# One engine instead of two for the lower parts of the second expert weights, after each change of expert

## The chip, the cores and the metric

The kernel runs on one core of a Trainium2 chip. The metric is the device time of one execution in microseconds, the median of several runs. Five engines work side by side on the core, each with an instruction queue of its own that it follows in order: TensorE (in the rows PE, its weight loads PEld), VectorE (DVE), ScalarE (ACT), GpSimd (POOL) and SyncE (SP), which here issues most of the DMAs. GpSimd issues the gathers and scatters by index as DMAs of its own. An engine waits for another through semaphores.

## The reference

The program is a chain of three parts, on float32 data:

```python
attn_out = _attn_ref(q, k, v)                 # 8 batches, 8 heads, 576 rows, 64 columns
x = attn_out.transpose(0, 2, 1, 3).reshape(4608, 512)

# mixture of experts: 8 experts, w1[e] is 512 x 1024, w2[e] is 1024 x 512
do_compute = x @ w_skip > 0
xc = x[do_compute]
e_idx = np.argmax(xc @ w_gate, axis=1)        # each row goes to one expert
for e in range(8):
    h = np.maximum(xc[e_idx == e] @ w1[e], 0.0)
    y[e_idx == e] = gate_w * (h @ w2[e])
out[do_compute] = xc + y

# then a rational MLP over all 4608 rows: g = P(x @ w_in) / Q(x @ w_in); g @ w_out
```

Only the part with the experts is touched by the change.

## The kernel before

A float32 product is made on TensorE in three passes: each operand is split into a higher part (rounded to the type that TensorE reads at its full rate) and a lower part, the difference; the passes are higher x higher, higher x lower and lower x higher. The helper `split(hi, lo, s, on_pool)` does it: ScalarE casts `s` to `hi` (L835), and then VectorE, or GpSimd if `on_pool` is set, subtracts `hi` from `s` into `lo` (L837).

The rows of the experts are sorted into slots of 256 rows, at most 25 slots (`MAXS`), each of one expert. `slot(i, kd, ch)` is emitted once for each slot, under run-time branches: `kd` says whether both halves of 128 rows are filled (2, a full slot) or one (1, a half slot), and `ch` what comes after it: 0, the same expert stays; 1, another expert follows; 2, this was the last one. A slot goes like this:

- gathers of the gates (L930, GpSimd);
- layer 1 on TensorE (L870, in a half slot L904 with transposes at L913), the relu and its split into `hh` and `hl` (L876 and L877, in a half slot L835 and L837); in a full slot also layer 2 of the second half (`layer2(1, ...)`, L886) and its store (L893 on VectorE, the scatter L894 on GpSimd);
- the transposes of the next slot's rows (L855) and their split into `xth` and `xtl`;
- gathers of the rows of the slot after that (L849, GpSimd);
- layer 2 of the first half (`layer2(0, ...)`, L886);
- if the expert stays: two pairs of blocks of the MLP's weights are loaded and converted (L796 to L813), around the store;
- if it changes: `split_w1` for eight blocks of 128 columns, from the staging tile `hold` into `w1h` and `w1l`; then the store; then `split_w2` for eight blocks, from the staging tile `w2s` into `w2h` and `w2l`; then `load_next(i + 1)`, by which SyncE loads the expert after the next into `hold` (L827) and `w2s` (L832, 2 MB each).

So the weights of an expert are loaded while the slots of the one before are computed, and split at the change. `w2s` can be loaded anew only when all eight blocks are split. In layer 2 the passes of a block f are `hh` x `w2h`, `hh` x `w2l` and `hl` x `w2h`, in this order (L885). Within the sections of a slot the order on each engine is that of the code (`tc.manual_schedule()`).

Which engine subtracts for `w2l` is decided in `split_w2`: VectorE the blocks 0, 2, 4, 6 and GpSimd the blocks 1, 3, 5, 7. It is called at two places: once before the first slot's work (L973), and at each change of expert (L1016). With 8 experts there are 7 changes.

Of the kernel before, what the change touches and what calls it, by code (L numbers as in the profile page):

```python
# [128 lines left out]
def load_block(nc, hold, xd, b):  # L129
    return nc.sync.dma_start(out=held_x(hold), in_=xd[b * TB:(b + 1) * TB, :].rearrange("(p j) d -> p j d", p=P))  # L130


def load_in(nc, hold, wc_in, f2):
    nc.sync.dma_start(out=held_wi(hold, f2), in_=wc_in[:, f2 * 2 * P:(f2 + 1) * 2 * P].rearrange("(k p) f -> p k f", p=P))
# [646 lines left out]
def experts(tc, w1, w2, w_in, w_out, wc_in, wc_out, xd, gd, ident, logits, sidx, gates, etab, xtab, kind, change, pair, early, hold, xts, hr, wos, w2s, phs, ahead, hs, av, ab, R, dbg=None):  # L781
# [5 lines left out]
    with ExitStack() as st:  # L787
# [6 lines left out]
        def convert_load(c, u):  # L794
            for m in range(2):
                nc.sync.dma_start(out=raws[2 * u + m], in_=src[m][:, c])  # L796

        def convert(c, u):
            parts = []
            for m in range(2):  # L800
                lo, hi = raws[2 * u + m][:, 0, :, 0], raws[2 * u + m][:, 0, :, 1]
                sq = cv.tile([P, CW], F32, name=f"cvs{m}")
                nc.scalar.activation(sq, hi.bitcast(F32), AF.Square)  # L803
                parts.append((lo, hi, sq, cv.tile([P, CW], I32, name=f"cvt{m}")))
            for lo, hi, sq, t in parts:
                nc.vector.tensor_scalar(out=t, in0=hi, scalar1=3, scalar2=0x3FFFFFFF, op0=ALU.logical_shift_left, op1=ALU.bitwise_and)
            for lo, hi, sq, t in parts:
                nc.vector.scalar_tensor_tensor(out=t, in0=hi, scalar=-0x40000000, in1=t, op0=ALU.bitwise_and, op1=ALU.bitwise_or)
            for lo, hi, sq, t in parts:
                nc.vector.scalar_tensor_tensor(out=t, in0=lo, scalar=29, in1=t, op0=ALU.logical_shift_right, op1=ALU.bitwise_or)  # L810
            for m, (lo, hi, sq, t) in enumerate(parts):
                nc.vector.scalar_tensor_tensor(out=sq, in0=sq, scalar=2.0 ** -30, in1=t.bitcast(F32), op0=ALU.is_ge, op1=ALU.mult)
                nc.sync.dma_start(out=dst[m][:, c], in_=sq.unsqueeze(1))  # L813
# [4 lines left out]
        w2h, w2l = wp.tile([P, KF, DM], F32R, name="w2h"), wp.tile([P, KF, DM], F32R, name="w2l")  # L818
# [15 lines left out]
        def split(hi, lo, s, on_pool):  # L834
            nc.scalar.copy(hi, s)  # L835
            eng = nc.gpsimd if on_pool else nc.vector
            eng.tensor_tensor(out=lo, in0=s, in1=hi.bitcast(F32), op=ALU.subtract)  # L837

        def split_w1(c, on_pool):
            sl = (slice(None), slice(None), slice(c * P, (c + 1) * P))  # L840
            split(w1h[sl], w1l[sl], w1s[sl], on_pool)

        def split_w2(f):
            split(w2h[:, f, :], w2l[:, f, :], w2s[:, f, :], f % 2 == 1)

        def gather(i):
            for a in range(2):
                col = 2 * i + a
                g = nc.gpsimd.indirect_dma_start(xrow[i % 3][a], None, xd, bass.IndirectOffsetOnAxis(ap=sidx[:, col:col + 1], axis=0), bounds_check=NT - 1, oob_is_err=False)  # L849
                tc.declare_no_dep(g.ins, group="scatters", reason="every slot reads and writes rows of its own")  # L850
# [28 lines left out]
        def layer2(a, hh, hl, py=None):  # L879
            if py is None:  # L880
                py = ps["y"][a]
            ts_ = slice(a * P, (a + 1) * P)
            n = 0
            for f in range(KF):
                for h, w in ((hh, w2h), (hh, w2l), (hl, w2h)):  # L885
                    nc.tensor.matmul(out=py, lhsT=h[:, f, ts_], rhs=w[:, f, :], start=(n == 0), stop=(n == 3 * KF - 1))  # L886
                    n += 1
            return py
# [31 lines left out]
        def get(tab, i, top):  # L920
            return nc.values_load(tab[0:1, i:i + 1], min_val=0, max_val=top, skip_runtime_bounds_check_because="the table holds sums of results of comparisons")

        def pair_at(i, u):
            c = nc.values_load(pair[0:1, 1 + u, i:i + 1], engines=[ET.SP], min_val=0, max_val=NPAIR - 1, skip_runtime_bounds_check_because="the table holds numbers of pairs, bounded by a minimum")
            return bass.ds(c, 1)

        def gather_gates(i):
            for a in range(2):
                col = 2 * i + a
                nc.gpsimd.indirect_dma_start(gates[:, col:col + 1], None, gd, bass.IndirectOffsetOnAxis(ap=sidx[:, col:col + 1], axis=0), bounds_check=NT - 1, oob_is_err=False)  # L930

        def load_next(i):
            e = expert(xtab, i, [ET.SP])
            load_w1(e)
            load_w2(e)
# [6 lines left out]
        def part1_full(i, hh, hl):  # L942
            for f2 in range(KF // 2):
                relu(f2, layer1(i, f2), hh, hl)
            if i == 0:
                tables()
            pts = [transposes(i + 1, a) for a in range(2)] if i < MAXS - 1 else []
            py = layer2(1, hh, hl)
            for a, pt in enumerate(pts):
                split_x(i + 1, a, pt)  # L950
            return store(i, 1, py)

        def part1_half(i, hh, hl):
            last = i == MAXS - 1
            r = []
            for g in range(2):
                r.append(layer1_half(i, g))
            pts = []
            for g in range(2):
                split_half(g, turn_half(g, r[g]), hh, hl)  # L960
                if not last:
                    pts.append(transposes(i + 1, g))
            for a, pt in enumerate(pts):
                split_x(i + 1, a, pt)
            if i == 0:
                tables()

        def slot(i, kd, ch):
            last = i == MAXS - 1
            if i == 0:  # L970
                with tc.manual_schedule():
                    for f in range(KF):
                        split_w2(f)  # L973
            with tc.manual_schedule():
                gather_gates(i)
            hh, hl = hp.tile([P, KF, SLOT], F32R, name="hh"), hp.tile([P, KF, SLOT], F32R, name="hl")
            with tc.If(kd > 1) as full:
                with tc.manual_schedule():
                    stored = part1_full(i, hh, hl)
            with full.Else():  # L980
                with tc.manual_schedule():
                    part1_half(i, hh, hl)
            with tc.manual_schedule():
                if i + 2 < MAXS:
                    gather(i + 2)
                py = layer2(0, hh, hl)
                if i > 0:
                    cs = [pair_at(i, u) for u in range(2)]
                with nullcontext() if last else tc.If(ch < 1) as stays:
                    if i > 0:  # L990
                        for u in range(2):
                            convert_load(cs[u], u)
                        convert(cs[0], 0)
                if not last:
                    with stays.Else():
                        with tc.If(ch < 2) as changes:
                            for c in range(8):
                                split_w1(c, False)
                        if i > NPAIR // 2:
                            with changes.Else(), tc.If(get(early, i, 1) > 0):  # L1000
                                x = load_block(nc, hold, xd, 0)
                                for f2 in range(2):
                                    load_in(nc, hold, wc_in, f2)
                                split_ahead(nc, hold, ahead)
                w = store(i, 0, py)
                if NPAIR // 2 < i < MAXS - 1:
                    why = "the block was loaded because no row of this slot belongs to it"
                    tc.declare_no_dep(x.ins, stored.ins, reason=why)
                    tc.declare_no_dep(w.ins, x.ins, reason=why)
                with nullcontext() if last else tc.If(ch < 1) as stays:  # L1010
                    if i > 0:
                        convert(cs[1], 1)
                if not last:
                    with stays.Else(), tc.If(ch < 2):
                        for f in range(KF):
                            split_w2(f)  # L1016
                        load_next(i + 1)

        with tc.manual_schedule():
# [256 lines left out]
```

## Time and profile before

| what | us |
|---|---|
| median of 3 runs | 1398.18 |
| lowest and highest of them | 1392.6 and 1401.56 |
| the profiled execution, device time | 1389.38 |
| its span from the first to the last instruction | 1387.7 |

All times of the rows below are of the profiled execution and counted from the start of its span. In that execution the experts' slots lie between about 175 and 550 us, attention before them and the MLP behind them.

### The profile page before, as it was taken

Reading aid. Unit: us, or ns where it says so; the run is one execution under the profiler, and the core shown is the slowest. Engines: PE = TensorE matmul, PEld = TensorE weight load, DVE = VectorE, ACT = ScalarE, POOL = GpSimd, SP = SyncE. Lnnn points to the kernel's source line nnn. Section 1 sums busy time; section 2 is a strip of 40 time slices with the busy share of each in tenths; the row PEclk is TensorE's granted clock in tenths of the full one; section 3 lists DMA queues with packets and bytes.
Section 4 is the critical chain, followed back from the end, with each engine's and each line's share of the span. In section 5 each row is a group of like instructions: output and inputs, shape, how many; then the busy total and the mean of one; then the engine's idle time right before and its main releaser. Section 6 shows DMA issues by size and latency. Waiting matters only on the chain.

```text
span 1387.7 us, 22256 instructions
## 1 busy us (share of the span) xinstructions
PE 1313.0 (95%) x7470; PEld 1190.3 (86%) x7470; DVE 1106.7 (80%) x2111; ACT 891.3 (64%) x1744; POOL 295.3 (21%) x247
## 2 busy tenths in 40 slices
PE   4989489898999998799999999999999999999998
PEld 3989478877998997789999999999999999999997
DVE  6998855766747664699888888888888889898887
ACT  2656235544243432699787878787877787878786
POOL 5756044556444442241000000000000000000000
PEclk9999789999999999899999999999999999999999
DMA  9984455667555654232000000000000000000000
GB/s 278 315 279 153 130 138 200 250 210 277 216 179 207 237 204 160 82 91 69 23 24 24 24 24 24 23 24 23 24 23 24 24 24 24 24 23 24 1 23 23
DMA packets 87063, 143.90 MB, mean 104 GB/s; under 512 B 22052, under 2 KB 52772, under 8 KB 85872
## 3 DMA queue, kind: packets, MB, share of 16 engines
q1 hardware_dynamic: 79824, 125.88, 27.5%
q0 software_dynamic: 7072, 16.06, 3.7%
q8 instruction: 72, 1.18, 0.3%
q14 instruction: 95, 0.78, 0.2%
HBM read 110.66 MB, written 35.15 MB: 105 GB/s over the span
## 4 chain that ended last, share of the span: by engine, by line
PE 56%; DVE 2%; ACT 0%; issue 0%; DVEq 0%
PE py L1219 28%; PE ph L1171 28%; PE pt L1150 1%; DVE w2s L1198 0%; DVE w2s L1206 0%; DVE gl L1200 0%; DVE w2s L1208 0%; DVE w2s L1204 0%; DVE w2s L1209 0%; DVE wi0l L1128 0%; DVE w2s L1202 0%; DVE r L1202 0%; ACT w2s L1190 0%; DVE xl L1128 0%; ACT w2s L1194 0%
## 5 line engine op out<-in xcount | busy, mean ns | idle before, releaser
L1219 PE MATMUL py<-woh,gh 128*128 128x512 f32 x576 | 227.7, 395 | 0.0
L1219 PE MATMUL py<-woh,gl 128*128 128x512 f32 x576 | 226.5, 393 | 0.1
L1219 PE MATMUL py<-wol,gh 128*128 128x512 f32 x576 | 225.9, 392 | 0.0
L1180 ACT CAST gh<-w2s 128x384 fp32r<-128x384 f32 x192 | 98.6, 513 | 139.4 <-PE py L1219 131.9
L1200 DVE TENSOR_TENSOR gl<-w2s,gh 128x384 fp32r<-128x384 f32 x192 | 110.1, 573 | 65.8 <-ACT gh L1180 65.8
L1190 ACT ACTIVATE w2s<-w2s,ab 128x384 f32<-128x384 f32 x190 | 135.1, 711 | 6.3
L1219 PEld LDWEIGHTS py<-woh,gl 128*128 128x128 f32 x576 | 108.0, 188 | 24.5 <-DVE gl L1200 1.2
L1191 ACT ACTIVATE w2s<-ph,av 128x384 f32<-128x384 f32 x190 | 124.4, 655 | 0.0
L1219 PEld LDWEIGHTS py<-wol,gh 128*128 128x128 f32 x576 | 108.3, 188 | 17.0
L1219 PEld LDWEIGHTS py<-woh,gh 128*128 128x128 f32 x576 | 108.2, 188 | 17.0 <-ACT gh L1180 0.5
L1209 DVE SCALAR_TENSOR_TENSOR w2s<-w2s,av,ph 128x384 f32<-128x384 f32 x190 | 116.9, 615 | 6.7
L870 PE MATMUL ph<-xth,w1h 128*128 128x256 f32 x416 | 118.1, 284 | 0.8 <-ACT xth L835 0.7
L870 PE MATMUL ph<-xtl,w1h 128*128 128x256 f32 x416 | 117.8, 283 | 0.1
L870 PE MATMUL ph<-xth,w1l 128*128 128x256 f32 x416 | 117.6, 283 | 0.0
L1204 DVE TENSOR_TENSOR w2s<-w2s 128x384 f32<-128x384 f32 x190 | 105.7, 556 | 13.9
L1208 DVE TENSOR_TENSOR w2s<-w2s,ph 128x384 f32<-128x384 f32 x190 | 103.8, 546 | 0.0
L886 PE MATMUL py<-w2h,hl 128*128 128x512 f32 x240 | 94.8, 395 | 8.2 <-DVE hl L877 8.2
L886 PE MATMUL py<-w2h,hh 128*128 128x512 f32 x240 | 95.8, 399 | 0.0
L886 PE MATMUL py<-w2l,hh 128*128 128x512 f32 x240 | 94.4, 393 | 0.7 <-POOL w2l L837 0.7
L1189 ACT ACTIVATE w2s<-ph 128x384 f32<-128x384 f32 x190 | 92.5, 487 | 0.0
L894 POOL DMA_INDIRECT xd<-y,sidx x30 | 56.3, 1876 | 167.3 <-DVE y L893 101.3
L803 ACT ACTIVATE cvs<-raw 128x512 f32<-128x512 f32 x32 | 21.3, 677 | 107.9 <-DMA wc_in<-cvs 44.1
(268 smaller groups left out, 3510.0 us busy)
## 6 DMA issues: line engine op xcount, KB each, us to landing
hold<-in_moe_w_dram SPq DMA_DIRECT2D x8, 2048.0 KB, 8.8
w2s<-in_moe_w_dram SPq DMA_DIRECT2D x8, 2048.0 KB, 9.8
hold<-xd SPq DMA_DIRECT2D x12, 768.0 KB, 4.2
out_dram<-o SPq DMA_DIRECT2D x36, 256.0 KB, 2.2
vm<-in_v_dram SPq DMA_DIRECT2D x8, 1024.0 KB, 7.4
qm<-in_q_dram SPq DMA_DIRECT2D x8, 1024.0 KB, 11.3
xd<-xs SPq DMA_DIRECT2D x8, 1024.0 KB, 4.2
raw<-in_moe_w_in_dram SPq DMA_DIRECT2D x16, 512.0 KB, 8.1
```

The source lines that it names most:

```text
L870: nc.tensor.matmul(out=ph[:, u, :], lhsT=a[:, k, fs], rhs=b[:, k, :], start=(n == 0), stop=(n == 3 * KD - 1))
L886: nc.tensor.matmul(out=py, lhsT=h[:, f, ts_], rhs=w[:, f, :], start=(n == 0), stop=(n == 3 * KF - 1))
L1171: nc.tensor.matmul(out=ph, lhsT=w[:, k, :], rhs=x[k // 2][:, k % 2, :], start=(n == 0), stop=(n == 3 * KD - 1))
L1180: nc.scalar.copy(gh, pn4)
L1189: nc.scalar.activation(m, ph, AF.Abs)
L1190: nc.scalar.activation(qq, m, AF.Identity, scale=ab[:, 1:2], bias=ab[:, 0:1])
L1191: nc.scalar.activation(pn, ph, AF.Identity, scale=av[:, 3:4], bias=av[:, 2:3])
L1200: GL(nc).tensor_tensor(out=gl, in0=pn4, in1=gh.bitcast(F32), op=ALU.subtract)
L1204: nc.vector.tensor_tensor(out=qq, in0=m, in1=qq, op=ALU.mult)
L1208: nc.vector.tensor_tensor(out=pn, in0=pn, in1=ph, op=ALU.mult)
L1209: nc.vector.scalar_tensor_tensor(out=pn, in0=pn, scalar=av[:, 1:2], in1=ph, op0=ALU.add, op1=ALU.mult)
L1219: nc.tensor.matmul(out=py, lhsT=g[:, ts_], rhs=w[:, f, :], start=(f == 0 and n == 0), stop=(f == KF - 1 and n == 2))
```

## The change

`split_w2` gets the blocks that GpSimd takes as an argument. The call before the first slot passes (1, 3, 5, 7), as it was; the call at a change of expert passes none, so VectorE subtracts for all eight blocks there and GpSimd for none. Nothing else changes.

```diff
-        def split_w2(f):
-            split(w2h[:, f, :], w2l[:, f, :], w2s[:, f, :], f % 2 == 1)
+        def split_w2(f, on_pool):
+            split(w2h[:, f, :], w2l[:, f, :], w2s[:, f, :], f in on_pool)
...
                     for f in range(KF):
-                        split_w2(f)
+                        split_w2(f, (1, 3, 5, 7))
...
                         for f in range(KF):
-                            split_w2(f)
+                            split_w2(f, ())
                         load_next(i + 1)
```

## Rows read from the trace of the kernel before

**Rows 1.** The page's head, and its busy times of the engines.

```profile
span 1387.7 us, 22256 instructions
PE 1313.0 (95%) x7470; PEld 1190.3 (86%) x7470; DVE 1106.7 (80%) x2111; ACT 891.3 (64%) x1744; POOL 295.3 (21%) x247
```

**Rows 2.** TensorE's waits from 200 to 545 us: total, times, longest.

```profile
PE py L886 <- DVE hl L877: 8.2, 2, 4.6
```

**Rows 3.** Timeline of TensorE: start, duration, what ran; [idle before, releaser].

```profile
254.38 0.40 PE L886 MATMUL py<-w2l,hh 128*128 128x512 f32 x1
258.43 0.50 PE L886 MATMUL py<-w2h,hl 128*128 128x512 f32 x1 [3.65 <-DVE hl L877]
...
332.14 0.40 PE L886 MATMUL py<-w2l,hh 128*128 128x512 f32 x1
337.13 0.79 PE L886 MATMUL py<-w2h,hl 128*128 128x512 f32 x1 [4.59 <-DVE hl L877]
```

**Rows 4.** Timeline of VectorE ahead of these two gaps.

```profile
249.30 0.69 DVE L837 TENSOR_TENSOR w2l<-w2s,w2h 128x512 fp32r<-128x512 f32 x1 [2.89 <-ACT w2h L835]
250.29 7.48 DVE L837 TENSOR_TENSOR w2l<-w2s,w2h 128x512 fp32r<-128x512 f32 x3 [0.29 <-ACT w2h L835]
...
327.18 0.69 DVE L837 TENSOR_TENSOR w2l<-w2s,w2h 128x512 fp32r<-128x512 f32 x1 [2.29 <-ACT w2h L835]
...
330.25 6.22 DVE L837 TENSOR_TENSOR w2l<-w2s,w2h 128x512 fp32r<-128x512 f32 x1 [0.35 <-ACT w2h L835]
```

**Rows 5.** Timeline of GpSimd in the same two stretches.

```profile
249.96 1.02 POOL L894 DMA_INDIRECT xd<-y,sidx  x1 [5.33 <-DMA x<-xd,sidx]
251.00 5.01 POOL L837 TENSOR_TENSOR w2l<-w2s,w2h 128x512 fp32r<-128x512 f32 x4
...
330.97 4.94 POOL L837 TENSOR_TENSOR w2l<-w2s,w2h 128x512 fp32r<-128x512 f32 x4
```

**Rows 6.** Timeline of ScalarE in the first of them.

```profile
248.59 4.27 ACT L835 CAST w2h<-w2s 128x512 fp32r<-128x512 f32 x8 [4.31 <-DMA w2s<-in_moe_w_dram]
252.76 2.04 ACT L876 ACTIVATE hh<-ph 128x512 fp32r<-128x512 f32 x4
```

**Rows 7.** Windows behind the second gap, L886 alone: us, PE and PEld busy, granted clock, DMA.

```profile
337.13:341.93 4.80, 4.80 (x11) 3.80 (x12) 0.50 0.82 260
341.93:345.35 3.42, 3.42 (x16) 2.79 (x15) 1.00 1.02 376
```

**Rows 8.** Timeline of TensorE in the second of these windows.

```profile
341.97 0.39 PE L886 MATMUL py<-w2l,hh 128*128 128x512 f32 x1
...
345.19 0.39 PE L886 MATMUL py<-w2h,hh 128*128 128x512 f32 x1
```

**Rows 9.** Instructions on the tile w2s, 200 to 545 us: ns least/median/most, first and last start.

```profile
L837 POOL TENSOR_TENSOR w2l<-w2s,w2h x28: 1267/1297/1316, 233.8 to 464.6; 128x512 fp32r<-128x512 f32 x28
```

**Rows 10.** A change into a full slot: timelines of VectorE and of TensorE.

```profile
270.94 2.49 DVE L837 TENSOR_TENSOR w2l<-w2s,w2h 128x512 fp32r<-128x512 f32 x4
...
281.09 0.48 PE L886 MATMUL py<-w2h,hh 128*128 128x512 f32 x1
```

**Rows 11.** A change into a half slot: timelines of VectorE and of TensorE.

```profile
309.21 2.49 DVE L837 TENSOR_TENSOR w2l<-w2s,w2h 128x512 fp32r<-128x512 f32 x4
313.82 1.48 DVE L837 TENSOR_TENSOR hl<-ph,hh 128x512 fp32r<-128x512 f32 x2 [2.12 <-ACT hh L835]
...
314.69 0.40 PE L886 MATMUL py<-w2h,hl 128*128 128x512 f32 x1
```

**Rows 12.** The other such change: timelines of VectorE, GpSimd and SyncE.

```profile
230.36 2.49 DVE L837 TENSOR_TENSOR w2l<-w2s,w2h 128x512 fp32r<-128x512 f32 x4
...
230.72 3.00 POOL L894 DMA_INDIRECT xd<-y,sidx  x1 [4.26 <-DVE y L893]
233.75 5.02 POOL L837 TENSOR_TENSOR w2l<-w2s,w2h 128x512 fp32r<-128x512 f32 x4
...
238.80 0.37 SPq L832 DMA_DIRECT2D w2s<-in_moe_w_dram  x1
```

## The prediction

> **What bounds the kernel now.** I began with the page's head: TensorE is busy for 95% of the span [rows 1], so a change on VectorE and GpSimd can only pay where TensorE waits for them. The second view is therefore TensorE's waits, cut to the stretch in which experts change. There it waits twice for the lower part of the relu, `hl` on VectorE, 8.2 us together [rows 2]. Everything else that the change touches lies beside a busy TensorE.
>
> The timelines show what stands behind the two waits. TensorE makes the first two passes of layer 2, starts the second at 254.38 and 332.14, and begins the third, which reads `hl`, only at 258.43 and 337.13 [rows 3]. `hl` is not late because of ScalarE: in the first stretch its `hh` are made from 252.76 on [rows 6]. It is late because it stands on VectorE's queue behind the subtracts for `w2l`, and one of these is stretched. A subtract takes 0.69 us; the three from 250.29 on take 7.48, and the one from 330.25 on takes 6.22 alone [rows 4]. In the same time GpSimd runs its four subtracts, 251.00 to 256.01 and 330.97 to 335.91 [rows 5]. The second stretched subtract ends at 336.47, half a microsecond after GpSimd's last. So the two engines, both subtracting tiles of the SBUF, shut each other out, and the one that is in goes on until its queue has a hole. Here VectorE had holes (0.29 and 0.35 us of idle time, waiting for ScalarE's casts [rows 4]), since it takes only every second block; GpSimd got in with a scatter at 249.96 and kept the way with its subtracts [rows 5].
>
> Both places have the same history: the change into a half slot just before them freed `w2s` late, the next load landed late (ScalarE's casts wait for that DMA [rows 6]), and so the split ran shortly ahead of layer 2, not well ahead of it.
>
> A third cost hangs on the second gap: the granted clock is 0.50 from 337.13 to 341.93 and 1.00 behind that [rows 7]. TensorE had stood idle for 4.59 us before it [rows 3].
>
> **The change part by part.** *Moved work.* At 7 changes GpSimd loses 28 subtracts of 1.297 us [rows 9], 36.3 us. VectorE gets them at a pitch of (2.49 - 0.69) / 3 = 0.60 us [rows 10], 28 x 0.60 = 16.8 us more. What that is worth depends on the place.
>
> *First gap.* VectorE starts at 249.30 [rows 4]. ScalarE's casts come every 0.52 us (4.27 for eight, the last about 0.62 [rows 6]), faster than 0.60, so VectorE has no hole any more and GpSimd's subtracts are gone. Eight subtracts end at 249.30 + 7 x 0.60 + 0.69 = 254.19, the first `hl` at 254.88. Without any wait the third matmul would come a pitch of (345.19 - 341.97) / 14 = 0.23 us [rows 8] after 254.38, at 254.61. It came at 258.43, so 3.55 to 3.82 us are won.
>
> *Second gap.* The same from 327.18: the subtracts end at 332.07, `hl` at 332.76, against 332.37 without a wait and 337.13 before. Won: 4.37 to 4.76 us.
>
> *Where in these bounds.* SyncE's load of `w2s` waits for the last subtract of a change. At 230.36 that was GpSimd's, which ended at 238.77; the load was issued at 238.80 [rows 12]. VectorE alone would end at 230.36 + 4.20 + 0.69 = 235.25, so the load is issued 3.5 us sooner and may land 0 to 3.5 us sooner (the load into `hold`, issued ahead of it, may still be running). Landing 0.4 us sooner is enough to close both gaps fully. I take the upper ends, 3.82 + 4.76 = 8.58 us, since the chip has 3.5 us to find 0.4 in; the lower ends give 7.92.
>
> *Clock.* From 337.13 to 341.97 there are 11 steps of matmuls in 4.84 us; at 0.23 they take 2.53. So 2.31 us were lost to the lower level (1.2 instead of 2.4 GHz), and with the gap closed I see nothing left that would bring it on. Bounds 0 and 2.31; I take 2.31, as the windows around it stand at 1.00.
>
> *Changes into a half slot.* Here `hl` comes soon after the split. At 309.21 eight subtracts end at 314.10, and `hl`, which began at 313.82, begins 0.28 us later. It ends at 314.79, and the third matmul, at 314.69 before [rows 11], slips by 0.10 us. For the other half slot 0 to 0.28. I take 0.10 in all.
>
> *Changes into a full slot.* At 270.94 eight subtracts end at 275.83; layer 2 begins at 281.09 [rows 10]. Layer 1 covers the 2.4 us that are added. Cost nothing; without the cover 4 x 0.60 = 2.40 each.
>
> *GpSimd's queue.* Behind the store's scatter and the subtracts stand the gathers of gates and rows for the next slots. A scatter that met VectorE's subtracts took 3.00 us (230.72 to 233.72), against 1.02 at another place, and ended 0.87 us after the last of them [rows 5, 12]. With eight subtracts it would end at 235.25 + 0.87 = 236.1, and the gathers follow at once; before, they stood behind 238.77. So the gathers come 2.6 us sooner and the scatter 2.4 us later. Nobody reads what it writes before the MLP part. Cost nothing.
>
> *The scatter as the one that comes first.* At 249.96 it did take the way [rows 5]. If it does so again, VectorE's subtracts start up to 1.02 us later at each of the two places: 0 to 2.04 us. I take 0, because the sooner load moves the subtracts away from layer 2 by more than that. The Trainium skill (SBUF — State Buffer, section Who interferes with whom) says that issue order decides which of the two engines blocks, and that the second one blocks until the first has finished; the stretched subtracts agree, 6.22 us against 0.69. By that rule a scatter that is issued first at both places costs its whole length, and the sum would be 8.8 instead of 10.8.
>
> *Sum.* 8.58 + 2.31 - 0.10 = 10.8 us; with all lower ends 7.92 + 0 - 0.56 - 2.04 = 5.3. Against the profiled execution's 1389.38 that gives 1378.6. This execution lies 8.8 us below the median of the runs shown, and below the lowest of them; on the median of 1398.18 the forecast is 1387.4, a ratio of 0.992.
>
> **The rivals.** *Nothing moves (1398).* The subtracts were stretched by something other than GpSimd's, or another wait takes the place of `hl`: the gaps stay. For it: the releaser of the holes is ScalarE, and the load that made the split late is still there. Against it: both stretched subtracts end with GpSimd's fourth, and where VectorE had finished before GpSimd began, as at 230.36 [rows 12], four take their 2.49.
>
> *The clock falls more often in the timed runs (1385).* In the profiled execution the clock fell after the second gap and not after the first, of 3.65 us. In the timed runs, all longer than it, it may have fallen after both. Then 2 x 2.31 are won: 8.58 + 4.62 - 0.10 = 13.1 us. Nothing in this trace shows it; the distance of 8.8 us leaves room.
>
> *VectorE becomes the bound at the changes (1404).* VectorE carries 2.4 us more at each change, all of it ahead of `hl`. Were `hl` the last thing that layer 2 waits for at all 7, that costs 7 x 2.4 = 16.8 us, and with the 10.8 won the kernel is 6.0 us slower. The point from which it decides is an `hl` that stands less than 2.4 us ahead of its matmul. That is so at the half slots (0.18 us [rows 11]), where the delay itself is only 0.28; at the full slots 5 us lie between [rows 10].
>
> **How the numbers follow.** The forecast gets 0.70, nothing moves 0.10, the clock 0.12, the bound 0.08. The forecast's own range is 5.3 to 10.8 us won, 1387.4 to 1392.9, and the runs before spread from 5.6 below to 3.4 above their median, so a median of some runs may lie a few microseconds off. The range goes from 1381 (the clock's case and this scatter) to 1397; it leaves out the bound and most of the case in which nothing moves. About 1% of 1398 is what a measurement of this kernel can tell from no change, so faster begins at 1384.2: most of the clock's case comes near it and about a tenth of the forecast's may pass it, together 0.17. Slower begins at 1412, which even the bound only reaches with a bad spread: 0.04. The rest, 0.79, is within 1%.
>
> **What would show it.** In the profile after: no stretched subtract for `w2l` at the changes, 56 of them on VectorE there at 0.69 us; no wait of TensorE for `hl` over 1 us; the granted clock at 1.00 through the stretch that was at 0.50; SyncE's loads of `w2s` some 3 us sooner behind each half slot's split; scatters of some 5 us at the changes and no subtract of GpSimd there except in the first slot. The prediction is wrong if a wait for `w2h` or for `x` stands where `hl` stood, if gathers of GpSimd stretch the subtracts in its subtracts' place, or if the stretch from 200 to 545 us shortens and the MLP part gives the time back.

## The result, and the profile after

The changed kernel takes 1379.8 us, median of 7 runs (1377.44 to 1384.8); the kernel before, timed beside it, 1393.31 us (7 runs, 1390.11 to 1401.56). The ratio is 0.9906 with a 95% interval of 0.9884 to 0.9929: 13.1 us won, 9.9 to 16.2. The forecast was 10.8 us won and 1387.4 us, with a range from 1381 to 1397. The gain lies inside the interval; the time lies 1.2 us below the range.

The page of the changed kernel begins like this:

```profile
span 1380.5 us, 22251 instructions
PE 1310.9 (95%) x7470; PEld 1189.9 (86%) x7470; DVE 1110.8 (80%) x2139; ACT 890.5 (65%) x1744; POOL 274.8 (20%) x219
```

28 instructions have gone from GpSimd to VectorE, as against [rows 1]. GpSimd's busy time falls by 20.5 us, less than 28 x 1.297 = 36.3, because its scatters take longer (72.2 us in all against 56.3). VectorE's rises by 4.1 and not by 16.8: the 11.1 us by which two subtracts had been stretched (6.28 and 6.22 less 0.69 each) were counted as busy too. That leaves 5.7; where the other 1.6 us went is open.

TensorE's waits from 200 to 536 us, to be laid beside [rows 2]:

```profile
PE ph L870 <- ACT cvs L803: 1.3, 1, 1.3
PE py L886 <- DVE hl L837: 0.2, 1, 0.2
PE ph L913 <- ACT hr L907: 0.2, 1, 0.2
```

The 8.2 us of waiting for `hl` behind L877 are gone. Timelines of VectorE, GpSimd and TensorE at the place of the first gap, which answer to [rows 3 to 5]:

```profile
249.74 4.93 DVE L837 TENSOR_TENSOR w2l<-w2s,w2h 128x512 fp32r<-128x512 f32 x8 [2.10 <-ACT w2h L835]
254.60 1.87 DVE L877 SCALAR_TENSOR_TENSOR hl<-ph,hh 128x512 fp32r<-128x512 f32 x3
...
249.61 1.02 POOL L894 DMA_INDIRECT xd<-y,sidx  x1 [5.97 <-DMA x<-xd,sidx]
250.94 1.03 POOL L930 DMA_INDIRECT gates<-gd,sidx  x1 [0.31 <-issue]
...
256.57 0.39 PE L886 MATMUL py<-w2l,hh 128*128 128x512 f32 x1
256.80 0.40 PE L886 MATMUL py<-w2h,hl 128*128 128x512 f32 x1
```

Eight subtracts take 4.93 us without a hole, the first `hl` is done at 255.28, 1.5 us ahead of its matmul, and the third matmul follows the second after 0.23 us. The scatter that got there first (249.61) did not hold the subtracts up. Counted from the slots' starts, the loads of `w2s` ahead of the two places were issued 3.5 and 3.4 us sooner (3.5 had been worked out), and the splits there began 1.7 and 1.4 us sooner.

The granted clock through both places, windows of the changed kernel (us; busy times and counts of PE, PEld, DVE, ACT, POOL; clock; DMA), against 0.50 in [rows 7]:

```profile
249.00:262.00 13.00, 13.00 (x90) 12.04 (x89) 8.52 (x14) 11.56 (x22) 6.01 (x5) 1.00 0.89 315
322.00:341.00 19.00, 18.02 (x109) 15.77 (x108) 9.68 (x16) 7.55 (x15) 7.47 (x6) 1.00 0.91 329
```

The new line among the waits, ScalarE's `cvs`, is the first cast of a conversion (L803). The experiments show that it is more than a remainder.

**Slot by slot.** TensorE begins a slot with the first matmul of its layer 1 (L870 or L904). The differences between neighbours, taken from TensorE's timeline, give each slot's length; all others agree within 0.4 us:

| execution | slot 0 | slot 3 | slot 5 | slot 7 | slot 8 |
|---|---|---|---|---|---|
| before, the profile of the prediction | 26.6 | 27.0 | 14.8 | 29.9 | 23.1 |
| after | 27.2 | 23.1 | 13.1 | 24.6 | 22.8 |

The first gap lies in slot 3 (3.9 us won), the second in slot 7 (5.3 us). Slot 5 gives 1.7 us that were not forecast. These are one execution each; the repeats below show how far they vary.

### The profile page after: what moved, and what is told of

Same layout as the page of the kernel before. It is cut to its first block, busy times and chain, and to the rows that moved or that the text cites. A ratio compares the mean times of both kernels' runs of the same rounds, so it can differ in the third digit from the quotient of the medians.

```text
span 1380.5 us, 22251 instructions
## 1 busy us (share of the span) xinstructions
PE 1310.9 (95%) x7470; PEld 1189.9 (86%) x7470; DVE 1110.8 (80%) x2139; ACT 890.5 (65%) x1744; POOL 274.8 (20%) x219
## 4 chain that ended last, share of the span: by engine, by line
PE 57%; DVE 1%; ACT 1%; issue 0%; ACTq 0%
PE ph L1171 28%; PE py L1219 28%; PE pt L1150 1%; DVE gl L1200 0%; DVE w2s L1198 0%; DVE w2s L1206 0%; DVE w2s L1204 0%; ACT w2s L1190 0%; ACT gh L1180 0%; DVE w2s L1208 0%; DVE wi0l L1128 0%; ACT w2s L1189 0%; ACT w2s L1191 0%; ACT wi0h L1127 0%; DVE w2s L1202 0%
## 5 line engine op out<-in xcount | busy, mean ns | idle before, releaser
L1219 PEld LDWEIGHTS py<-woh,gl 128*128 128x128 f32 x576 | 108.1, 188 | 24.5 <-DVE gl L1200 1.2
L870 PE MATMUL ph<-xth,w1h 128*128 128x256 f32 x416 | 118.1, 284 | 2.0 <-ACT cvs L803 1.3
L870 PE MATMUL ph<-xtl,w1h 128*128 128x256 f32 x416 | 118.0, 284 | 0.1
L870 PE MATMUL ph<-xth,w1l 128*128 128x256 f32 x416 | 117.8, 283 | 0.0
L894 POOL DMA_INDIRECT xd<-y,sidx x30 | 72.2, 2405 | 176.2 <-DVE y L893 148.7
L886 PE MATMUL py<-w2h,hh 128*128 128x512 f32 x240 | 94.9, 396 | 0.0
L886 PE MATMUL py<-w2l,hh 128*128 128x512 f32 x240 | 93.6, 390 | 0.4 <-POOL w2l L837 0.4
L886 PE MATMUL py<-w2h,hl 128*128 128x512 f32 x240 | 93.8, 391 | 0.2 <-DVE hl L837 0.2
L803 ACT ACTIVATE cvs<-raw 128x512 f32<-128x512 f32 x32 | 21.3, 680 | 100.2 <-DMA wc_in<-cvs 53.0
## 6 DMA issues: line engine op xcount, KB each, us to landing
w2s<-in_moe_w_dram SPq DMA_DIRECT2D x8, 2048.0 KB, 11.1
```

Of the source, the lines that this page charges most:

```text
L870: nc.tensor.matmul(out=ph[:, u, :], lhsT=a[:, k, fs], rhs=b[:, k, :], start=(n == 0), stop=(n == 3 * KD - 1))
L1219: nc.tensor.matmul(out=py, lhsT=g[:, ts_], rhs=w[:, f, :], start=(f == 0 and n == 0), stop=(f == KF - 1 and n == 2))
```

## The experiments

The theories: **A**, GpSimd's subtracts stretch VectorE's, and with them the relu's lower part; **B**, it is the sooner load of `w2s` that closes the gaps; **C**, something at the other changes gives part of the gain; and, formed after the first four runs, **D**: behind the gap stood a second bound, the conversions' loads (of the MLP's weights), which stand behind the load of `w2s` in SyncE's queue.

### VectorE alone at the two changes with gaps, or at the other five

```diff
-                            split_w2(f, ())
+                            split_w2(f, () if i in (2, 6) else (1, 3, 5, 7))
```

> VectorE alone only at the two changes at which the kernel before had a gap (the ends of slots 2 and 6); at the other five GpSimd subtracts the blocks 1, 3, 5, 7 as before. Theory A (GpSimd's subtracts stretch VectorE's): the subtracts at these two places take 0.69 us each, the load of the staging tile is not sooner, so 0.3 to 0.5 us are left of each gap, the clock stays at 1.00, and about 10 us are won against the kernel before. Theory B (the sooner load is what closes the gaps): the gaps stay at 3.7 and 4.6 us, nothing is won. Theory C (something else at the other five changes gives part of the 13.5 us): 10 us here and the rest in the run with the other five.

Measured: ratio 0.9933 (0.9913 to 0.9954), 9.3 us won. The longest of the 36 subtracts on VectorE takes 0.73 us. Of the gaps none and 0.46 us are left, the clock stays at 1.00. That is 0.7 us short of A's 10. B as the only cause is out.

```diff
-                            split_w2(f, ())
+                            split_w2(f, (1, 3, 5, 7) if i in (2, 6) else ())
```

> The complement: VectorE alone at the five changes without a gap, GpSimd takes 1, 3, 5, 7 at the ends of slots 2 and 6. Theory A: subtracts are stretched at the two places again, but start 1.4 to 1.8 us sooner because the load lands sooner; the gaps shrink to about 2 and 3 us, the clock may or may not fall, 3 to 6 us are won. Theory B: both gaps are closed, 10 to 11 us are won. Theory C: 3 us or more are won with gaps as before.

Measured: ratio 0.9943 (0.9924 to 0.9963), 7.9 us won. VectorE's timeline at the first place:

```profile
249.84 6.67 DVE L837 TENSOR_TENSOR w2l<-w2s,w2h 128x512 fp32r<-128x512 f32 x3 [0.29 <-ACT w2h L835]
```

TensorE's waits from 184 to 536 us, two of the lines:

```profile
PE py L886 <- DVE hl L877: 3.1, 2, 1.9
PE ph L870 <- ACT cvs L803: 1.9, 1, 1.9
```

Three subtracts that need 1.9 us take 6.67: A's stretch is there as before. But 7.9 us are more than A's 3 to 6, though the interval (5.2 to 10.6) reaches into that. The two runs give 17.2 us together where the change gives 13.1; the three intervals leave room for a plain sum. That the remedies cover the same wait in part is seen in the profiles: slot 3, 27.0 us before, is 23.1 in the run with the two changes and 24.5 here. Slot 7 is 27.3 us long here, slot 5 12.8.

### GpSimd keeps its four subtracts, but the last ones

```diff
-                            split_w2(f, ())
+                            split_w2(f, (4, 5, 6, 7))
```

> GpSimd subtracts four blocks again at every change, but 4 to 7 instead of 1, 3, 5, 7, so VectorE has its four one behind the other. Theory A with holes (GpSimd gets in where VectorE waits for ScalarE between its blocks): VectorE has no hole, its four subtracts take 2.5 us and the relu's lower part follows at once; both gaps are gone up to 0.5 us although GpSimd does as much as before: 8 to 11 us won. Theory A without holes (whenever both have subtracts to do, VectorE loses): one subtract is stretched to some 6 us and the gaps stay: 0 won. Theory B: the load is as late as before, 0 won.

Measured: ratio 1.0003 (0.9986 to 1.0019), nothing won. But not because the gaps had stayed. Timelines of VectorE, SyncE, ScalarE and TensorE of this kernel in slot 7:

```profile
329.18 2.50 DVE L837 TENSOR_TENSOR w2l<-w2s,w2h 128x512 fp32r<-128x512 f32 x4 [4.28 <-ACT w2h L835]
...
336.57 0.37 SPq L832 DMA_DIRECT2D w2s<-in_moe_w_dram  x1
339.21 0.35 SPq L796 DMA_DIRECT2D raw<-in_moe_w_in_dram  x1
...
348.72 0.66 ACT L803 ACTIVATE cvs<-raw 128x512 f32<-128x512 f32 x1 [13.08 <-issue]
...
344.35 0.39 PE L886 MATMUL py<-w2h,hl 128*128 128x512 f32 x1
349.44 0.58 PE L870 MATMUL ph<-xth,w1h 128*128 128x256 f32 x1 [4.70 <-ACT cvs L803]
```

None of the 28 subtracts on VectorE takes more than 0.69 us, so A's holes are right: with four blocks one behind the other GpSimd doesn't get in. `hl` is on time; TensorE waits 1.2 us for `hh`. Then it stands 4.70 us at the end of the slot, until ScalarE has begun the conversion. The row doesn't name what ScalarE waited for, but the blocks are loaded (L796) behind `w2s` (L832), which is issued when the last subtract is done, and the packets of the trace follow this order: 95% of the load's packets (2048 bytes each) had ended at 344.4, and the first of the blocks' packets (4096 bytes) started at 343.8. The clock falls to 0.50 with this wait, as it did after the other one. A window of this kernel:

```profile
347.00:353.80 6.80, 4.36 (x20) 4.36 (x21) 4.36 (x8) 1.36 (x2) 0.00 (x0) 0.50 0.70 260
```

So this run refuted what I expected of A, and theory D came from it.

### Less and less left to GpSimd

The same edit with one block and with two:

```diff
-                            split_w2(f, ())
+                            split_w2(f, (7,))      # the other run: (6, 7)
```

> As the changed kernel, but at every change GpSimd subtracts block 7. Theory D (behind the gap there was a second bound: ScalarE's first cast of a conversion starts some 12.3 us after the load into the staging tile is issued, and TensorE's next slot waits for it): in slot 7 the load is issued some 1.5 us later than in the changed kernel (12 us after the slot's start instead of 10.7), the cast starts at 24.5, the slot takes 25 us instead of 23.6 to 24.6, and 1 to 2 us of the gain are lost: 1381 to 1382. Theory A alone (only stretched subtracts cost): no stretch, 1379.8 as before.

> GpSimd subtracts blocks 6 and 7 at every change. Theory D: the load is issued some 13 us after the start of slot 7, the cast starts at 25.5, the slot takes 26.5 us or, where the clock falls, 28; slot 4 begins to wait too; 3 to 5 us of the gain are lost: 1383 to 1385, between the run with no block and the one with four (1393.1). Theory A alone: 1379.8.

Measured: ratio 0.9943 (0.9924 to 0.9961) and 0.9951 (0.993 to 0.9971), medians 1385.86 and 1386.36 us beside 1394.26 for the kernel before. No stretch at the changes, and yet 5.2 and 6.3 us of the gain are lost: A alone is out. D has the direction, but one block costs more than the 1 to 2 us expected, partly in slot 5 (14.8 us) and in slot 8 (24.7 us, the clock at 0.50 from 341.2 to 344.5 behind a wait of 2.62 us for `cvs`), which I had not counted. With two blocks the first slot, not edited, happened to have a gap of 4.0 us for `hl`.

The whole series in slot 7, in us after the slot's start: when the load of `w2s` is issued, when the first conversion's cast starts, and the slot's length.

| kernel | load issued | cast starts | slot 7 |
|---|---|---|---|
| after, second profile | 10.6 | 22.9 | 23.6 |
| after | 10.7 | 23.9 | 24.6 |
| VectorE alone at two changes | 12.3 | 24.7 | 25.4 |
| GpSimd block 7 | 12.8 | 25.2 | 25.9 |
| GpSimd blocks 6, 7 | 13.5 | 25.7 | 26.4 |
| VectorE alone at the other five | 14.2 | 26.6 | 27.3 |
| GpSimd blocks 4 to 7 | 16.6 | 28.7 | 29.4 |
| before, third repeat | 16.8 | 29.0 | 29.7 |
| before, second repeat | 17.0 | 29.2 | 29.9 |
| before, first repeat | 17.1 | 29.4 | 30.1 |
| before | 16.6 | 28.8 | 29.9 |

The cast starts 12.1 to 13.2 us after the load is issued, and the slot ends 0.7 us after the cast's start, down to the undisturbed 23.1. Only the last row lies off it (1.1): there `hl` and the clock set the end, and the conversion would have been ready at almost the same moment. Two waits lay upon each other. The repeats of the kernel before are described below. In the changed kernel the same chain reads, on the timelines of SyncE, ScalarE and TensorE:

```profile
327.49 0.37 SPq L832 DMA_DIRECT2D w2s<-in_moe_w_dram  x1
...
340.64 0.66 ACT L803 ACTIVATE cvs<-raw 128x512 f32<-128x512 f32 x1 [10.80 <-DMA raw<-in_moe_w_in_dram]
...
341.35 0.38 PE L870 MATMUL ph<-xth,w1h 128*128 128x256 f32 x1 [1.34 <-ACT cvs L803]
```

Issued 10.7 us after the slot's start at 316.76, the load leaves TensorE 1.34 us to wait.

### The kernel before three times, the changed one once more

No edit.

> The kernel before, unchanged, to see where its executions differ: the one profiled so far took 1389.4 us, shorter than nearly all timed ones. Theory A alone: the same gaps for the relu's lower part (3.7 and 4.6 us), the clock at 0.50 after the second only; what differs lies outside the experts. Theory A with the clock: in a longer execution the clock falls after the first gap too, 2.3 us more.

> The kernel before once more, with the same two expectations: the gaps as in the first profile and differences outside the experts, or the clock at 0.50 after the first gap too.

> The kernel before a third time, with the same two expectations: the gaps as in the first profile and differences outside the experts, or the clock at 0.50 after the first gap too.

> The changed kernel, unchanged: no gap for the relu's lower part, the experts' stretch within 1 us of the 361.5 us of the first profile; if what differs between executions lies outside the experts, attention, the turn to the MLP and the MLP differ by up to some 3 us each.

Measured: 1394.1, 1399.26 and 1388.45 us for the kernel before, 1377.94 for the changed one. The stretch of the experts, from the first transpose (L855) to the last matmul of layer 2 (L886), worked out from TensorE's timeline:

| execution | experts | slot 0 | slot 3 | slot 5 | slot 7 | slot 8 |
|---|---|---|---|---|---|---|
| before | 372.1 | 26.6 | 27.0 | 14.8 | 29.9 | 23.1 |
| first repeat | 375.1 | 25.4 | 29.7 | 14.0 | 30.1 | 25.1 |
| second repeat | 378.7 | 31.1 | 28.5 | 14.1 | 29.9 | 24.5 |
| third repeat | 372.0 | 25.7 | 29.2 | 14.0 | 29.7 | 22.8 |
| after | 361.5 | 27.2 | 23.1 | 13.1 | 24.6 | 22.8 |
| after again | 359.9 | 26.3 | 23.1 | 13.1 | 23.6 | 22.8 |

The executions of the kernel before differ inside the experts, by up to 6.7 us, and by up to 4.1 us outside them. So the first expectation, that the gaps stay as they were and all that differs lies outside, is refuted. The MLP alone takes 817.1 to 817.2 us in all four of before and 816.5 in both of after. In all three repeats the clock falls after the first gap too. Windows of the third repeat behind its gap of 3.03 us:

```profile
256.40:262.20 5.80, 5.80 (x14) 4.54 (x15) 2.84 (x5) 2.18 (x4) 2.84 (x3) 0.50 0.88 284
262.40:264.00 1.60, 1.60 (x8) 1.30 (x7) 0.00 (x0) 0.00 (x0) 0.00 (x0) 1.00 0.91 318
```

Slot 3 is 1.5 to 2.7 us longer there than in the profile that I forecast from. In the first repeat, and in the second too, VectorE had finished its four subtracts in slot 7 before GpSimd got in, so `hl` was on time. TensorE's timeline at the slot's end in the first:

```profile
343.79 0.39 PE L886 MATMUL py<-w2h,hl 128*128 128x512 f32 x1
350.60 0.58 PE L870 MATMUL ph<-xth,w1h 128*128 128x256 f32 x1 [6.42 <-ACT cvs L803]
```

The slot took 30.1 us all the same, without any edit: D's wait stood where A's had been. In the second repeat the wait was 6.33 us and the slot took 29.9. So of four executions of the kernel before two waited in slot 7 for `hl` (4.59 and 4.80 us) and two for the conversion, and the slot is 29.7 to 30.1 us long in all four. Behind the two waits for the conversion the clock is at 0.50, and slot 8 is the longer for it (25.1 and 24.5 us). And the second repeat has the stretch in slot 0, which the change leaves as it was. Its timelines of VectorE and TensorE:

```profile
193.02 6.06 DVE L837 TENSOR_TENSOR w2l<-w2s,w2h 128x512 fp32r<-128x512 f32 x1 [0.35 <-issue]
...
199.73 0.79 PE L886 MATMUL py<-w2h,hl 128*128 128x512 f32 x1 [3.87 <-DVE hl L877]
```

The means of the experts' stretch are 374.5 for before and 360.7 for after, 13.8 us apart. That is as much as the timed runs gained (13.5 us between the medians), though four and two executions are few. By slots it is 5.5 us in slot 3, 5.8 in slot 7, 1.1 in slot 5, 1.1 in slot 8 and 0.5 in slot 0, which the change leaves as it was.

### VectorE alone in the first slot too

```diff
-                        split_w2(f, (1, 3, 5, 7))
+                        split_w2(f, ())
```

> The change, and VectorE alone in the first slot too. All theories: as the changed kernel at the changes. In the first slot TensorE's wait for GpSimd's first block goes (0.4 us), and the table work on VectorE is not stretched by GpSimd (3.7 us for one small instruction becomes 0.4), so the first load of weights is issued some 2 us sooner. 0 to 1 us more than the changed kernel, so 13 to 14 us against the kernel before.

Measured: ratio 0.9902 (0.9883 to 0.9922), median 1380.22 us (5 runs, 1379.02 to 1381.09). That is the changed kernel's ratio, 0.9906, within both intervals. The 0 to 1 us more that were expected are not shown: the first slot takes 27.6 us in its profile, no less than the 27.2 and 26.3 of the changed kernel. Its runs lie closer together, which fits a first slot that can no longer be stretched; five runs don't prove it.

### The conversions' loads in a queue of their own

```diff
-                nc.sync.dma_start(out=raws[2 * u + m], in_=src[m][:, c])
+                nc.scalar.dma_start(out=raws[2 * u + m], in_=src[m][:, c])
```

Besides, the numbers of the pairs are loaded for ScalarE too (L924). Once with GpSimd on blocks 4 to 7:

> GpSimd subtracts blocks 4 to 7 as in the run that gained nothing, but the loads for the conversions are issued by ScalarE instead of SyncE, so they don't stand behind the load of the weights in SyncE's queue. Theory D: ScalarE's first cast no longer keeps to 12.3 us after the weight load's issue, the two waits for it (2.3 and 4.7 us) shrink below 1.5 us, and 6 to 10 us are won against the kernel before. Rival: the DMA engines are what is short, not the queue's order: the waits stay and nothing is won.

Measured: ratio 0.9994 (0.9973 to 1.0014). Nothing is won, and D's 6 to 10 us are a miss. Slot 7 does shrink to 23.2 us, but slot 5 grows to 20.2 and slot 8 to 28.2. ScalarE's waits from 260 to 360 us, and two of TensorE's from 184 to 536, in this kernel:

```profile
ACT cvs L803 <- DMA w2s<-in_moe_w_dram: 20.2, 2, 12.1
...
PE ph L904 <- ACT cvs L803: 4.5, 1, 4.5
PE ph L870 <- DVE y L893: 3.1, 1, 3.1
```

So order in SyncE's queue alone isn't it; the casts now wait elsewhere. At the end of slot 4 the packets of the two loads run side by side: those of the blocks from 283.1 to 293.3 and those of `w2s` from 280.3 to 295.3, 15 us against 8.4 in slot 7 of the run with the same blocks. Whether the DMA engines or ScalarE's own order of issues and casts holds the casts is open.

And once with VectorE alone everywhere:

> VectorE alone everywhere, and the conversions' loads issued by ScalarE: the two remedies together. Theory D: the last 0.4 to 1.3 us of waits for ScalarE's first cast go, and the weight loads are a little slower by sharing: 1378 to 1381. Rival: ScalarE's queue is held up by issuing the loads, and TensorE waits for its relus: 1382 or more.

Measured: ratio 0.9893 (0.9866 to 0.992), median 1378.51 us (4 runs). No wait for `cvs` is left in its profile, as D has it; a difference to the changed kernel isn't shown.

## Why the prediction was wrong, and where it was right

The forecast was 7.6 us too long. Two steps of the sum failed, the base and the gain, and a miss of either size alone would have left the time inside the range, whose lower end lay 6.4 us below the forecast.

**The sum's anchor.** "On the median of 1398.18 the forecast is 1387.4": the base, a median of three runs, was off. Seven runs of the kernel before gave 1393.31, 28 runs later 1394.26. On 1393.31 the same 10.8 us give 1382.5. This is 4.9 of the 7.6 us.

**The gain.** The other 2.7 us are gain that the sum did not have: 13.5 us between the medians, not 10.8. By the slots' means over all profiles it is 5.5 us at the first gap (forecast 3.82, with no clock), 5.8 at the second (forecast 7.07, with the clock) and 2.2 in slots 5 and 8, for which the sum had no term. So it missed in its terms more than in its total.

**The clock.** "Bounds 0 and 2.31; I take 2.31" was sized from one execution with one fall. The repeats show the clock at 0.50 after the first gap as well, in three of three. The rival in which it falls more often (13.1 us won, 0.12) is the one whose condition came true, and its number too: 13.1 by the ratio. With it on the base of 1393.31 the sum gives 1380.2. That the number fits so well is partly luck: the rival has 13.2 us in slots 3 and 7, which give 11.3, and nothing in slots 5 and 8.

**First gap.** 3.55 to 3.82 us were forecast, slot 3 shrank by 3.9 in the profile. The size is right for an execution without the fall of the clock, and so is the mechanism: the stretch is back where GpSimd subtracts in VectorE's holes (the other five, slot 0 in a repeat) and gone where there are none (blocks 4 to 7). The upper end was the right choice, since the split began more than 0.4 us sooner.

**Second gap.** With the clock 4.76 + 2.31 = 7.07 us were forecast; slot 7 shrank by 5.3 and, in the second profile, by 6.3. The size was near, the reason was half of it. I entered the sooner load as 0 to 3.5 us that close a remainder of 0.4, and did not ask what was late next. A conversion stood right behind: closing the gap with the load as late as before is worth nothing (ratio 1.0003), and in two of four executions of the kernel before the gap for `hl` was not there at all, with the slot as long. That the change wins as much here takes both, VectorE without a stretch and the last subtract 5 to 6 us sooner in the slot (load at 10.7 against 16.6).

**Slot 5**, 1.7 us in the first profiles, was not in the sum. Before, TensorE waited 1.9 us there for `hr`, which is ScalarE's; after, 0.2 (the waits above). Before, among its waits from 200 to 545 us:

```profile
PE ph L913 <- ACT hr L907: 1.9, 1, 1.9
```

The load was issued 6.1 instead of 10.4 us into slot 4, whose conversions reach into slot 5. In the runs whose conversions are loaded by SyncE, slot 5 takes 12.8 to 13.1 us with the load at 6.1 to 6.6, 14.0 to 14.8 with it at 9.7 to 10.4, and 15.4, with slot 4 longer too, at 13.6 (blocks 4 to 7). So this part comes from the other five changes (12.8 us there, 14.5 with the two changes alone), as C had it, and it fits D; no run isolates the conversions from the rest of ScalarE's work.

**Half slots.** 0.10 us were forecast; the one wait for `hl` of L837 after is 0.2 us.

**GpSimd's queue.** The gathers did come sooner, and TensorE waited for no scatter. The scatter that came first, at 249.61, cost 0 and not 1.02 us, so the 8.8 that I made of the Trainium skill's rule (SBUF — State Buffer, section Who interferes with whom) did not come. The section states the rule for a VectorE instruction with two SBUF inputs beside a GpSimd instruction that reads SBUF. For GpSimd's subtracts the rows agree with it; that a scatter holds VectorE off for its whole length was my addition, and one row speaks against it. In the kernel before, the rows leave it open (last section).

**VectorE as the bound** did not happen at any change.

## What to carry to other kernels

Moving an instruction from a helper engine to a busy one can pay twice: it takes the stretch off the busy engine and frees the shared staging buffer sooner; ask for each wait that you remove which transfer is released by the same work, and what stands behind it in its queue. Two waits that lie upon each other look like one in a profile; the cheap test is to remove the first alone and see whether the time moves. Forecast against as many executions as there are: the base was off by 4.9 us with three, and a gap that sometimes brings the clock down can cost more in the median than in the one profile.

## What the runs showed of the hardware that I had not expected

- GpSimd's four subtracts, once in, are not interrupted: a VectorE subtract of 0.69 us takes up to 6.3 us. Eight VectorE subtracts without a hole, 4.93 us, are not interrupted either.
- GpSimd's scatters and gathers behave unevenly. Eight subtracts of VectorE kept their pitch of 0.60 us beside a scatter of 1.02 and a gather of 1.03 us, while some scatters, 3.00 us in [rows 12], last until shortly after VectorE's last subtract. And in all seven stretches of the kernel before's four profiles a scatter (in slot 0 a gather) was running when the stretched subtract began, 0.5 to 0.7 us ahead of GpSimd's first subtract; at 250.29 its own 0.69 us would have ended before that one at 251.00 [rows 4, 5]. What the scatter has to do with the stretch is open.
- Gaps of TensorE of 3.0 to 3.6 us were followed by the lower clock in all three repeats, the one of 3.65 us in the first profile was not. Waits for the conversion at the end of slot 7 show the same: behind 1.87 us (the other five) and 2.62 us (block 7) the clock was at 0.50, behind 3.14 us (blocks 6 and 7) at 1.00.
